# VectorE transposes k times its decay in blocks of 32 rows for the last 14 attention units, in place of TensorE's transposes and ScalarE's copy

## The chip, the cores and the metric

One core of a Trainium2 chip. The metric is the device time of one execution in microseconds (us), the median of several runs. The engines are TensorE (PE; its weight loads are listed as PEld), VectorE (DVE), ScalarE (ACT), GpSimd (POOL) and SyncE (SP), which issues the DMAs.

## The reference

Gated linear attention over 4 batches and 8 heads, and its output goes through a gated two-layer network:

```python
for t in range(S):                      # S = 768, D = 48, B = 4, H = 8
    state = alpha[:, :, t, :, None] * state + np.einsum('bhd,bhe->bhde', k[:, :, t], v[:, :, t])
    y[:, :, t] = np.einsum('bhd,bhde->bhe', q[:, :, t], state)
x = y.transpose(0, 2, 1, 3).reshape(B * S, H * D)          # 3072 x 384
gate = 1.0 / (1.0 + np.exp(-(x @ w_gate)))                 # 384 x 1536
out = (gate * (x @ w_val)) @ w_out                         # 1536 x 384
```

## The kernel before

The 3072 tokens are cut into 6 groups of 512. A group's attention is done in 4 units, one for each pair of heads, so there are 24 units, u = 0 to 23. The network is done in 72 steps, 12 for each group (one for each slice of 128 columns of the 1536). Every product of the network is taken three times with split operands, so a step is 27 matmuls of 128 by 128 by 512: nine for the gate (`pg`, L225), nine for the value (`pv`, L225), and six with `hh` and three with `hl` that add the step before into the three output banks (`po`, L643). For each step ScalarE takes the sigmoid (`sg`, L630), VectorE multiplies (L632), ScalarE writes the upper half `hh` (L634) and VectorE the lower half `hl` (L635). Gate and value use a ring of three PSUM banks, `r_three`, which the outputs of a unit share.

A unit of a later group runs while the network works on an earlier one. The first 8 units are `unit`, the others `late`. In `late` the two heads of a unit lie in rows 0 to 47 and 64 to 111 of a tile of 128 rows, with 512 tokens along it. VectorE scans the decays G (L381) and F (L385), GpSimd multiplies k by G in place (`kT`, L388), VectorE multiplies q by F into `A` (L549). `turn` then has TensorE transpose the four squares of 128 tokens of `kT` into the PSUM bank `pk` (L400), and ScalarE copies the bank to the tile `kn` (L404), which has the tokens along its rows. `scores` (L560) multiplies k and q, `adds` (L567) multiplies `kn` and v to give what each chunk of 64 tokens adds to the state. VectorE masks the scores (L573) and runs the states in eight dependent steps (L586), GpSimd scales them (L591). `outputs` of the unit (L603) come one unit later, right behind the next unit's `scores` and `adds`. ScalarE and VectorE take the outputs out of PSUM as `yt` (L422, L423), and DMAs from SP's queue put them in the tile `x` (L430), which the next group's gate and value products read.

The banks: `r_two` is a ring of two PSUM banks. A late unit takes three turns of it, the first for `pk` and two for `pas`, so `pk` and the second of `pas` are the same bank. `kn` is a ring of one tile once the early units have gone (`r_kn`), so a unit's `kn` can be written only when the `adds` of the unit before have read it.

The order of the work on each engine is set by a planner, class `Plan`. Every piece of work is given an engine, an estimated time, a due time (in steps of 6.12 us, from the dictionaries in `begin`) and what it reads and writes. The planner runs through time, and an engine that is free takes the piece with the earliest due time among those that are ready, where a piece's due time is also brought forward to what its users need. The network's pieces of steps after 14 that are marked `soon` go ahead of everything else. The order is then fixed, and each engine works through its list in that order. `last_step(u)` is the step beside which the outputs of unit u run, and y is three steps before it; the transposes are due at y - 0.5, the scores at y + 0.5, G of the next unit at y + 0.1.

Of the kernel before, what the change touches and what calls it, by code (L numbers as in the profile page):

```python
# [17 lines left out]
P = 128  # L18
# [18 lines left out]
CH, EH = T // C, T // E  # L37
X16 = R - D
PLACES = tuple((j * D + X16 * k, k, R * j + D, X16) for j in range(2) for k in range(NK)) + \
    tuple(((2 * p + j) * D, p - 1, R * j, D) for p in range(1, NP) for j in range(2))  # L40
EARLY = 2 * NP


WIDTH = EH + 3 * T + 1
# [143 lines left out]
def vec(n):  # L188
    return 0.07 + n / 960


def act(n):
    return 0.09 + n / 1180
# [35 lines left out]
def chunked(ctx, tc, rows, vc, vh, weights_in, out, const, ident, flags, weights, within):  # L229
    nc = tc.nc  # L230
    sb = ctx.enter_context(tc.tile_pool(name="sb", bufs=1))
    ps = ctx.enter_context(tc.tile_pool(name="ps", bufs=1, space=bass.MemoryType.PSUM))
    plan = Plan()
# [12 lines left out]
    def borrow(tag, *shape):  # L246
        t, at = slots[tag]
        size = 1
        for x in shape:
            size *= x  # L250
        slots[tag][1] = at + size
        name = f"{tag}_{at}"
        held[tag].append(name)
        t = t[:, at:at + size]
        if len(shape) == 2:
            t = t.rearrange("p (a b) -> p a b", b=shape[1])
        elif len(shape) == 3:
            t = t.rearrange("p (a b c) -> p a b c", b=shape[1], c=shape[2])
        return name, t
# [10 lines left out]
    def ring(name, n, *shape, dtype=F32, pool=None, early=()):  # L270
        return Ring([(f"{name}{i}", (pool or sb).tile([P, *shape], dtype, name=f"{name}{i}")) for i in range(n)], early)
# [5 lines left out]
    for _ in range(2):  # L277
        nm, t = borrow("w11", WF // 2, 2)
        raws.append((nm, t.bitcast(U32)))
    r_raw = Ring(raws)  # L280
    r_kn = ring("kn", 1, CH, P, early=[borrow("w6", CH, P) for _ in range(2)])
# [22 lines left out]
    r_two, r_three = Ring(r_at.tiles[:2]), Ring([*r_pg.tiles, *r_pv.tiles, r_at.tiles[2]])  # L304
# [9 lines left out]
    def later():  # L314
        nc.gpsimd.memset(d1g[E], 0.0)
        nc.gpsimd.memset(d1g[E][:, 0:T:E], 1.0)
        nc.gpsimd.memset(starts[:, 0:EARLY, CH:EH], 0.0)
        for lo in (0, E):
# [8 lines left out]
    plan.add("scalar", 0.7, None, picks, writes=[(pickn, "s")])  # L327
    plan.add("gpsimd", 1.5, NF - 4.0, later, writes=["later", *(("start", u) for u in range(EARLY))])

# [62 lines left out]
    def bound(u, t, fn, F):  # L392
        plan.add("scalar", act(T) + 0.22, t["flag"], lambda: nc.scalar.activation(
            out=F, in_=F, func=AF.Abs, accum_out=flags[:, u:u + 1]), writes=[fn, ("flag", u)])

    def turn(t, inn, kT, pkn, pk):

        def turned():
            for c in range(CH):
                nc.tensor.transpose(out=pk[:, c * P:(c + 1) * P], in_=kT[:, c * P:(c + 1) * P], identity=ident)  # L400

        plan.add("tensor", (0.109 * CH + 0.03, 0.9), t["X"], turned, [(inn, "k")], [pkn], fixed=True)
        knn, kn = r_kn.next()
        plan.add("scalar", act(CH * P), t["kn"], lambda: nc.scalar.copy(  # L404
            out=kn.rearrange("p c d -> p (c d)"), in_=pk[:, 0:CH * P]), [pkn], [knn])
        return knn, kn

    def finish(g, p, t, pyn, py):
# [26 lines left out]
    def unit(u, g, p, t):  # L435

        n, nch = T, CH
        bank = r_bank if u < NP else r_at
        inn, tin = r_in.next()
        for lo, hi, marks in ((0, A_K, "a"), (A_K, WIDTH, "rkq")) if u < 2 else ((0, WIDTH, "arkq"),):  # L440
            plan.add("sync", (0.475, P * (hi - lo) * 4 / RATE), t["load"], lambda lo=lo, hi=hi: nc.sync.dma_start(
                out=tin[:, lo:hi], in_=rows[g, p, :, lo:hi]), writes=[(inn, m) for m in marks])
        vn, v = r_v.next()
        plan.add("sync", (0.475, P * CH * 2 * D * 4 / RATE), after(t["load"], 0.2), lambda: nc.sync.dma_start(
            out=v.rearrange("p c j e -> p (c j e)"), in_=vc[g, p]), writes=[(vn, "v")])
        kT, qT = tin[:, A_K:A_Q], tin[:, A_Q:WIDTH]
# [3 lines left out]
            out=qT, in0=qT, in1=F, op=ALU.mult), [(inn, "r"), fn], [(inn, "q")], port=True)  # L450
        bound(u, t, fn, F)


        (pkn, pk), *pas = bank.next(), bank.next(), bank.next()
        knn, kn = turn(t, inn, kT, pkn, pk)

        def scores():
# [9 lines left out]
                                     start=True, stop=True)  # L467

        plan.add("tensor", (0.25 * nch + 0.1, 0.5), t["A"], scores, [(inn, "k"), (inn, "q")], [x[0] for x in pas])
        plan.add("tensor", (0.09 * nch + 0.1, 0.5), t["Y"], adds, [knn, (vn, "v")], [pkn])  # L470

        an, A = r_A.next()
        for j, (pan, pa) in enumerate(pas):
            plan.add("vector", vec(n), t["mask"], lambda pa=pa, j=j: nc.vector.tensor_tensor(
                out=A[:, j].rearrange("p (c t) -> p c t", t=C), in0=pa[:, 0:n].rearrange("p (c t) -> p c t", t=C),
# [17 lines left out]
        for lo in range(0, nch, some):  # L493
# [4 lines left out]
            out=sd, in0=st[:, 0:nch], in1=dec.rearrange("p (c o) -> p c o", o=1).broadcast_to([P, nch, D]), op=ALU.mult), [sn, decn], [(sdn, x) for x in range(4)])  # L498
# [30 lines left out]
    def late(u, g, p, t):  # L529


        inn, tin = r_in.next()
        plan.add("sync", (0.475, P * A_Q * 4 / RATE), t["load"], lambda: nc.sync.dma_start(
            out=tin[:, 0:A_Q], in_=rows[g, p, :, 0:A_Q]), writes=[(inn, m) for m in "ark"])
# [3 lines left out]
        for j in range(2):  # L538
            plan.add("sync", (0.475, R * T * 4 / RATE), after(t["load"], 0.1), lambda j=j: nc.sync.dma_start(
                out=A[own[j], j], in_=rows[g, p, own[j], A_Q:WIDTH]), writes=[(an, 2 + j)])  # L540
        plan.add("sync", (0.475, P * CH * 2 * D * 4 / RATE), after(t["load"], 0.2), lambda: nc.sync.dma_start(
            out=v.rearrange("p c j e -> p (c j e)"), in_=vc[g, p]), writes=[(vn, "v")])
        for j in range(2):
            plan.add("sync", (0.475, R * EH * D * 4 / RATE), after(t["load"], 0.3), lambda j=j: nc.sync.dma_start(
                out=vs[other[j], j].rearrange("p c e -> p (c e)"), in_=vh[g, p, j]), writes=[(vsn, j)])
        kT = tin[:, A_K:A_Q]
        fn, F, decn, dec = decays(u, E, t, inn, tin)
        for j in range(2):
            plan.add("vector", vec(T), t["q"], lambda j=j: nc.vector.tensor_tensor(  # L549
                out=A[own[j], j], in0=A[own[j], j], in1=F[own[j]], op=ALU.mult), [fn], [(an, 2 + j)], port=True)  # L550
        bound(u, t, fn, F)
        (pkn, pk), *pas = r_two.next(), r_two.next(), r_two.next()
        knn, kn = turn(t, inn, kT, pkn, pk)

        def scores():
            for c in range(EH):
# [10 lines left out]
                    nc.tensor.matmul(out=pas[c % 2][1][R * j:R * j + D, T // 2 + c // 2 * D:T // 2 + (c // 2 + 1) * D],  # L567
                                     lhsT=kn[ro, c // 2, R * j:R * j + D], rhs=v[ro, c // 2, j], start=True, stop=True)

        plan.add("tensor", (0.045 * EH, 0.5), t["Y"], adds, [knn, (vn, "v")], [x[0] for x in pas], fixed=True)  # L570
        for j, (pan, pa) in enumerate(pas):
            for i in range(2):
                plan.add("vector", vec(T // 2), t["mask"], lambda pa=pa, j=j, i=i: nc.vector.tensor_tensor(  # L573
                    out=A[other[j], j].rearrange("p (c i t) -> p i c t", i=2, t=E)[:, i],
# [5 lines left out]
        st, sn = sts[p], ("st", p)  # L580
        done = EH if u >= EARLY + NP else CH
        plan.add("gpsimd", 0.28, t["G"], lambda: nc.gpsimd.tensor_copy(out=st[:, 0, :], in_=st[:, done, :]), writes=[sn])
# [7 lines left out]
        for j in range(2):  # L590
            plan.add("gpsimd", pool_(EH * D), t["sd"], lambda j=j: nc.gpsimd.tensor_tensor(  # L591
                out=vs[own[j], j], in0=st[own[j], 0:EH], in1=dec[own[j]].rearrange("p (c o) -> p c o", o=1).broadcast_to([R, EH, D]), op=ALU.mult),
# [80 lines left out]
    def begin(u):  # L673
        g, p = divmod(u, NP)
        if u < EARLY:
            t = dict.fromkeys(("load", "G", "dec", "kt", "q", "X", "kn", "Y", "A", "mask", "S", "sd", "out", "y"))
            t.update(flag=14.0 + u, run=1, e_q="gpsimd")
        else:
            o = last_step(u)
            y = o - 3  # L680
            t = dict(load=y - 5, G=y - 2.9, dec=y - 2, kt=y - 2.7, flag=y + 1 + 0.5 * p, q=y - 2.0, X=y - 0.50, A=y + 0.50, kn=y - 1,
                     Y=y + 0.51, mask=y + 0.6, S=y + 0.55, sd=y + 0.7, out=o + 0.52, y=None)
        return unit(u, g, p, t) if u < EARLY else late(u, g, p, t)

# [12 lines left out]
    for s in range(NG * NF):  # L697
        step(s)
        if s in finished:
            u = finished[s]  # L700
# [6 lines left out]
    every, one, total = sb.tile([P, 1], F32, name="every"), sb.tile([P, 1], F32, name="one"), r_at.next()  # L707
    nc.vector.memset(one, 1.0)
    late, n_units = NG * NF - 4, NG * NP
    plan.add("scalar", 0.5, late, lambda: nc.scalar.activation(out=starts.rearrange("p u c -> p (u c)"), in_=starts.rearrange("p u c -> p (u c)"),  # L710
                                                               func=AF.Abs, accum_out=flags[:, n_units:n_units + 1]),
             [("start", x) for x in range(n_units)], [("flag", n_units)])
# [5 lines left out]
        out=within, in0=total[1][0:1, 0:1], scalar1=G_BOUND, scalar2=None, op0=ALU.is_le), [total[0]])  # L718
# [99 lines left out]
def laid_out(np, q, k, v, alpha, w_gate, w_val, w_out):  # L818
# [4 lines left out]
    for g in range(NG):  # L823
        size = C if g * NP < EARLY else E
        first[g, :, :, 0:T // size] = a[g, :, :, 0:T:size]
# [43 lines left out]
```

## Time and profile before

| | us |
|---|---|
| median of 3 runs | 556.48 (555.26 to 557.22) |
| the profiled execution | 556.98 |
| its span in the trace | 555.3 |
| TensorE busy in the span | 542.1 (98%) |
| VectorE busy | 335.0 (60%) |
| ScalarE busy | 183.9 (33%) |
| GpSimd busy | 100.5 (18%) |

The profile is of one execution; its span ends 1.7 us short of the time of its run. "Busy" is the time in which at least one instruction of the engine runs; for TensorE matmuls overlap, so its cost is read from start to start. Late units follow each other every 21.08 us.

### The profile page before, as it was taken

The numbers are of one execution on the slowest core, as the hardware profiler recorded it, in microseconds if no ns is written. First come the engines' busy times: TensorE is split into PE (matmuls) and PEld (weight loads), VectorE is DVE, ScalarE is ACT, GpSimd is POOL, SyncE is SP. The second block draws the span as 40 slices with busy tenths as digits, with TensorE's granted clock in tenths as the row PEclk, the third lists the DMA queues.
The fourth block names the chain that finished last, engine by engine and source line by source line (L and its number), as shares of the span: only waits on it lengthen the run. The fifth ranks groups of instructions, "written<-read, shape, count | busy, mean of one in ns | idle before, by whom it ended". The sixth has DMA issues, their size and how long they took to land.

```text
span 555.3 us, 10288 instructions
## 1 busy us (share of the span) xinstructions
PE 542.1 (98%) x4162; PEld 432.8 (78%) x4162; DVE 335.0 (60%) x648; ACT 183.9 (33%) x334; POOL 100.5 (18%) x133
## 2 busy tenths in 40 slices
PE   8999999999999999999999999999999999999994
PEld 4667776767888888888888888888888888888883
DVE  6889998899858457467467466476475342222221
ACT  2547767652322222322222322222332222221211
POOL 5711222142212112022022022022021010000000
PEclk9999999999999999999999999999999999999998
DMA  8537675644413213324124234024232011100001
GB/s 311 203 102 247 217 228 164 213 132 121 141 31 116 70 45 116 123 48 116 57 59 115 94 79 115 25 92 115 71 102 50 15 28 30 58 0 1 1 1 63
DMA packets 21449, 54.36 MB, mean 98 GB/s; under 512 B 3472, under 2 KB 8592, under 8 KB 21392
## 3 DMA queue, kind: packets, MB, share of 16 engines
q1 hardware_dynamic: 21392, 53.60, 31.6%
q8 instruction: 35, 0.57, 0.4%
q14 instruction: 22, 0.18, 0.1%
HBM read 41.01 MB, written 4.72 MB: 82 GB/s over the span
## 4 chain that ended last, share of the span: by engine, by line
PE 84%; DVE 6%; DMA 4%; ACT 3%; issue 1%; POOL 0%; SPq 0%; DVEq 0%; ACTq 0%; POOLq 0%
PE po L643 24%; PE pv L225 16%; PE pg L225 16%; PE at L225 15%; DMA raw<-in_w_dram 3%; PE pv L614 2%; PE at L560 2%; PE at L400 1%; PE pv L603 1%; PE at L567 1%; DVE w L355 1%; PE pg L603 1%; PE at L603 1%; DVE raw L351 1%; DMA first_w<-in_w_dram 1%
## 5 line engine op out<-in xcount | busy, mean ns | idle before, releaser
L225 PE MATMUL pg<-x,w 128*128 128x512 f32 x477 | 117.4, 390 | 0.0
L643 PE MATMUL po<-hh,w 128*128 128x512 f32 x432 | 115.7, 400 | 1.3 <-ACT hh L634 1.3
L225 PE MATMUL pv<-x,w 128*128 128x512 f32 x459 | 113.4, 391 | 0.7 <-DVE hl L635 0.7
L225 PEld LDWEIGHTS pg<-x,w 128*128 128x128 f32 x477 | 89.1, 188 | 19.1 <-issue 0.4
L225 PEld LDWEIGHTS pv<-x,w 128*128 128x128 f32 x459 | 85.5, 188 | 20.2 <-DVE hl L635 2.0
L643 PEld LDWEIGHTS po<-hh,w 128*128 128x128 f32 x432 | 78.2, 188 | 18.5 <-ACT hh L634 1.9
L225 PE MATMUL at<-x,w 128*128 128x512 f32 x360 | 88.3, 390 | 0.0
L225 PEld LDWEIGHTS at<-x,w 128*128 128x128 f32 x360 | 67.4, 188 | 14.2 <-issue 0.2
L591 POOL TENSOR_TENSOR vs<-st,dec 64x384 f32<-64x384 f32 x32 | 26.4, 827 | 213.0 <-DVE st L586 211.8
L643 PE MATMUL po<-hl,w 128*128 128x512 f32 x216 | 62.0, 392 | 0.0
L632 DVE TENSOR_TENSOR pv<-pv,sg 128x512 f32<-128x512 f32 x32 | 22.3, 697 | 53.9 <-PE pv L225 53.9
L388 POOL TENSOR_TENSOR in<-in,G 128x512 f32<-128x512 f32 x22 | 33.0, 1500 | 90.3 <-DVE G L381 42.1
L632 DVE TENSOR_TENSOR pg<-pg,sg 128x512 f32<-128x512 f32 x21 | 14.7, 699 | 56.2 <-PE pg L225 56.0
L643 PEld LDWEIGHTS po<-hl,w 128*128 128x128 f32 x216 | 40.2, 188 | 9.0 <-issue 0.4
L632 DVE TENSOR_TENSOR at<-at,sg 128x512 f32<-128x512 f32 x19 | 13.3, 699 | 53.0 <-PE at L225 53.0
L586 DVE SCALAR_TENSOR_TENSOR st<-st,dec,at 128x48 f32<-128x48 f32 x128 | 33.9, 265 | 8.4 <-PE at L567 3.0
L630 ACT ACTIVATE sg<-pg 128x512 f32<-128x512 f32 x32 | 19.2, 599 | 57.4 <-PE pg L225 57.4
L634 ACT CAST hh<-pv 128x512 fp32r<-128x512 f32 x32 | 18.9, 589 | 43.1 <-DVE pv L632 43.1
L630 ACT ACTIVATE sg<-at 128x512 f32<-128x512 f32 x21 | 12.6, 600 | 54.8 <-PE at L225 54.8
L630 ACT ACTIVATE sg<-pv 128x512 f32<-128x512 f32 x19 | 11.4, 600 | 52.5 <-PE pv L225 52.5
L381 DVE TENSOR_TENSOR_SCAN G<-in,d1g 128x512 f32<-128x512 f32 x22 | 26.7, 1215 | 2.0 <-DMA in<-in_rows_dram 1.8
L385 DVE TENSOR_TENSOR_SCAN F<-in,d1f 128x512 f32<-128x512 f32 x22 | 27.5, 1251 | 0.5
(158 smaller groups left out, 577.4 us busy)
## 6 DMA issues: line engine op xcount, KB each, us to landing
in<-in_rows_dram SPq DMA_DIRECT2D x16, 516.5 KB, 4.2
raw<-in_w_dram SPq DMA_DIRECT2D x12, 576.0 KB, 5.3
first_w<-in_w_dram SPq DMA_DIRECT2D x10, 576.0 KB, 5.0
x<-yt SPq DMA_DIRECT2D x30, 192.0 KB, 3.4
out_dram<-raw SPq DMA_DIRECT2D x18, 256.0 KB, 2.3
v<-in_vc_dram SPq DMA_DIRECT2D x22, 192.0 KB, 4.6
A<-in_rows_dram SPq DMA_DIRECT2D x32, 128.0 KB, 4.0
in<-in_rows_dram SPq DMA_DIRECT2D x4, 772.5 KB, 5.0
```

The costliest lines, as they stand in the source:

```text
L225: nc.tensor.matmul(out=dst, lhsT=lhs(a, i), rhs=rhs(b, i), start=(n == 0 and i == 0), stop=(n == len(todo) - 1 and i == NK - 1))
L381: plan.add("vector", scan(n), t["G"], lambda: nc.vector.tensor_tensor_scan(out=G[:, ::-1], data0=az[:, n:0:-1], data1=d1g[size], initial=0 ...
L385: plan.add("vector", scan(n), after(t["G"], 0.01), lambda: nc.vector.tensor_tensor_scan(out=F, data0=az[:, 0:n], data1=d1f, initial=0.0, o ...
L388: plan.add("gpsimd", pool_(n), t["kt"], lambda: nc.gpsimd.tensor_tensor(out=kT, in0=kT, in1=G, op=ALU.mult), [gn, (inn, "r")], [(inn, "k")])
L560: nc.tensor.matmul(out=pas[j][1][ro, c // 2 * E:(c // 2 + 1) * E], lhsT=kT[r, cs], rhs=A[r, j, cs], start=True, stop=True)
L586: nc.vector.scalar_tensor_tensor(out=st[:, c + 1, :], in0=st[:, c, :], scalar=dec[:, c:c + 1], in1=pas[c % 2][1][:, T // 2 + c // 2 * D:T ...
L591: plan.add("gpsimd", pool_(EH * D), t["sd"], lambda j=j: nc.gpsimd.tensor_tensor(out=vs[own[j], j], in0=st[own[j], 0:EH], in1=dec[own[j]]. ...
L603: nc.tensor.matmul(out=py[R * j:R * j + D, cs], lhsT=vs[r, j, c, :], rhs=A[r, j, cs], start=True, stop=True)
L630: plan.add("scalar", act(T), None, lambda: nc.scalar.activation(out=sg, in_=got["g"][1][:, 0:T], func=AF.Sigmoid), [got["g"][0]], [sgn], s ...
L632: plan.add("vector", vec(T), None, lambda: nc.vector.tensor_tensor(out=pv, in0=pv, in1=sg, op=ALU.mult), [sgn], [pvn], soon=soon)
L634: plan.add("scalar", act(T), None, lambda: nc.scalar.copy(out=hh, in_=pv), [pvn], [hhn], soon=soon)
L643: nc.tensor.matmul(out=pso_now[m][1][:, 0:T], lhsT=weights.part("o", b, f)[:, m * P:(m + 1) * P], rhs=h[a][:, 0:T], start=(f == 0 and i == ...
```

## The change

For units 10 to 23 `turn` isn't called. The tile `kn` is written by VectorE itself, straight from `kT`: for each block of 32 rows of `kT` (`a`) and each block of 32 tokens within the squares of 128 (`b`), one transpose instruction reads 32 rows by 4 by 32 elements and writes 32 rows by 4 by 32 elements; that is 16 instructions for a unit, put into the plan as four pieces of four. Units 0 to 9 keep TensorE's transposes and ScalarE's copy. A unit of the 14 takes two turns of the bank ring and not three. The plan is told of 4 x (0.07 + 128/960) us = 0.81 us for each piece.

```diff
+TURNED = 2
@@ turn
         plan.add("scalar", act(CH * P), t["kn"], lambda: nc.scalar.copy(
-            out=kn.rearrange("p c d -> p (c d)"), in_=pk[:, 0:CH * P]), [pkn], [knn])
+            out=kn.rearrange("p c d -> p (c d)"), in_=pk[:, 0:CH * P]), [pkn], [(knn, a) for a in range(4)])
@@ unit (and in the same way late): adds
-        plan.add("tensor", (0.09 * nch + 0.1, 0.5), t["Y"], adds, [knn, (vn, "v")], [pkn])
+        plan.add("tensor", (0.09 * nch + 0.1, 0.5), t["Y"], adds, [*((knn, a) for a in range(4)), (vn, "v")], [pkn])
@@ late
-        (pkn, pk), *pas = r_two.next(), r_two.next(), r_two.next()
-        knn, kn = turn(t, inn, kT, pkn, pk)
+        if u < EARLY + TURNED:
+            (pkn, pk), *pas = r_two.next(), r_two.next(), r_two.next()
+            knn, kn = turn(t, inn, kT, pkn, pk)
+        else:
+            pas = r_two.next(), r_two.next()
+            knn, kn = r_kn.next()
+            blocks = kT.rearrange("p (c q t) -> p q c t", q=4, t=32)
+            for a in range(4):
+                def turned(a=a):
+                    for b in range(4):
+                        nc.vector.transpose(out=kn[32 * b:32 * b + 32, :, 32 * a:32 * a + 32], in_=blocks[32 * a:32 * a + 32, b])
+
+                plan.add("vector", 4 * vec(P), t["X"], turned, [(inn, "k")], [(knn, a)], port=False)
```

## Rows read from the trace of the kernel before

**Rows 1.** The page: busy time by engine, and the chain that ended last
```profile
PE 542.1 (98%) x4162; PEld 432.8 (78%) x4162; DVE 335.0 (60%) x648; ACT 183.9 (33%) x334; POOL 100.5 (18%) x133
PE 84%; DVE 6%; DMA 4%; ACT 3%; issue 1%; POOL 0%; SPq 0%; DVEq 0%; ACTq 0%; POOLq 0%
```
**Rows 2.** Busy time by stretch, one late unit each; then PEclk, DMA share, GB/s
```profile
168.20:189.28 21.08, 21.08 (x189) 17.41 (x189) 12.56 (x26) 5.36 (x10) 4.07 (x5) 1.00 0.25 76
...
379.00:400.08 21.08, 21.08 (x184) 17.25 (x185) 13.16 (x27) 6.44 (x12) 3.75 (x4) 1.00 0.37 113
```
**Rows 3.** Timeline of PE, 412 to 446 us: start, time, engine, line
```profile
412.42 2.21 PE L225 MATMUL at<-x,w 128*128 128x512 f32 x9
414.47 0.60 PE L400 MATMUL at<-ident,in 128*128 128x128 f32 x4
414.82 1.63 PE L643 MATMUL po<-hh,w 128*128 128x512 f32 x6
416.30 0.84 PE L643 MATMUL po<-hl,w 128*128 128x512 f32 x3
...
421.66 0.54 PE L567 MATMUL at<-v,kn 64*48 64x48 f32 x32
...
427.38 2.20 PE L225 MATMUL pv<-x,w 128*128 128x512 f32 x9
429.42 1.52 PE L643 MATMUL po<-hh,w 128*128 128x512 f32 x6
430.77 0.84 PE L643 MATMUL po<-hl,w 128*128 128x512 f32 x3
```
**Rows 4.** Groups by line: ACT's copy (busy, mean ns, idle before)
```profile
L404 ACT COPY kn<-at 128x512 f32<-128x512 f32 x21 | 12.4, 591 | 33.2 <-PE at L400 33.2
```
**Rows 5.** Timeline of DVE, one period; in brackets the idle time before
```profile
401.15 2.43 DVE L586 SCALAR_TENSOR_TENSOR st<-st,dec,at 128x48 f32<-128x48 f32 x8 [0.21 <-PE at L567]
403.50 0.68 DVE L635 TENSOR_TENSOR hl<-pg,hh 128x512 fp32r<-128x512 f32 x1
...
405.97 0.69 DVE L423 TENSOR_TENSOR yt<-pv,yt 128x512 fp32r<-128x512 f32 x1
406.58 1.22 DVE L381 TENSOR_TENSOR_SCAN G<-in,d1g 128x512 f32<-128x512 f32 x1
...
410.11 0.69 DVE L635 TENSOR_TENSOR hl<-pg,hh 128x512 fp32r<-128x512 f32 x1
...
414.74 0.70 DVE L632 TENSOR_TENSOR at<-at,sg 128x512 f32<-128x512 f32 x1 [2.37 <-PE at L225]
416.21 0.69 DVE L635 TENSOR_TENSOR hl<-at,hh 128x512 fp32r<-128x512 f32 x1 [0.77 <-ACT hh L634]
421.32 0.70 DVE L632 TENSOR_TENSOR pv<-pv,sg 128x512 f32<-128x512 f32 x1 [4.42 <-PE pv L225]
```
**Rows 6.** Timeline of POOL in the same period: k times its decay
```profile
408.02 1.50 POOL L388 TENSOR_TENSOR in<-in,G 128x512 f32<-128x512 f32 x1 [2.87 <-DVE G L381]
```
**Rows 7.** Groups by line and shape: DVE instructions of other sizes
```profile
L387 DVE TENSOR_TENSOR dec<-in,G 128x8 f32<-128x8 f32 x16 | 2.6, 164 | 0.0
L573 DVE TENSOR_TENSOR A<-at,mask 64x256 f32<-64x256 f32 x64 | 27.0, 422 | 1.1
L549 DVE TENSOR_TENSOR A<-A,F 64x512 f32<-64x512 f32 x32 | 22.5, 702 | 0.5
```
**Rows 8.** Timeline of all engines at the end of a group's attention
```profile
216.10 0.69 DVE L423 TENSOR_TENSOR yt<-pv,yt 128x512 fp32r<-128x512 f32 x1
216.82 1.18 SPq L430 DMA_DIRECT2D x<-yt  x2
220.50 2.28 PE L225 MATMUL pv<-x,w 128*128 128x512 f32 x9
220.91 1.45 PEld L225 LDWEIGHTS pv<-x,w 128*128 128x128 f32 x7 [0.21 <-issue]
```
**Rows 9.** Line L430 in 210 to 225 us: from issue to landing
```profile
DMA to landing us min/median/max: 3.2/3.3/3.4
```

## What the change will do to the time

> **What bounds the kernel now.** First the busy times and the chain that ended last: TensorE is busy for 98% of the span and makes 84% of the chain; VectorE is busy for 60% [rows 1]. These are means over unlike stages, so the second view is the busy time by stretches. I cut the stretch from 168 to 442 us at the period of the late units, 21.08 us; it gives 13 stretches, and they hold the transposes of all but the first of the 14 units that change, which stand in the period ahead. In every one TensorE is busy for the whole 21.08 us at a granted clock of 1.00, while VectorE is busy for 12.56 us, or up to 13.16 us in the periods where it also copies a result out [rows 2]. So in this region time is TensorE's instruction stream and nothing else: an instruction taken out of it shortens the kernel by its own spacing, and one put on another engine costs nothing as long as TensorE isn't made to wait. The third view is the timeline of TensorE, for that spacing; the fourth that of VectorE, for the holes that have to take the new work.
>
> **What is removed.** Durations of matmuls overlap, so I read from start to start across the same three blocks, once with the transposes and once without. With them, from the first product of the nine at 412.42 to the first `hl` product at 416.30: 3.88 us. Without them, 427.38 to 430.77: 3.39 us [rows 3]. The difference is 0.49 us; of it 0.35 us lie between the first transpose (414.47) and the next product (414.82), and the rest is a slower change-over around them. The periods at 343 to 353 and 427 to 438 us, read in the same way, give 0.48. For 14 units: 14 x 0.48 = 6.7 us off TensorE's stream. ScalarE loses a copy of 0.59 us a unit [rows 4]. ScalarE is busy for 5.4 us of 21 [rows 2], so this is worth nothing in time. The shared PSUM bank and the third turn of the ring go too; no wait in this region comes from them, since TensorE has no idle time there, so they are worth nothing either.
>
> **What is added.** 16 transpose instructions a unit on VectorE, each over 32 rows and 128 elements a row. No instruction of that kind is in the trace, so the price c of one, from start to start, is bounded by its neighbours. Below: an instruction of 8 elements takes 0.164 us, nearly all of it fixed cost. Above: 512 elements a row take 0.702 us; in between, 256 elements read from PSUM take 0.422 us [rows 7]. The line from 8 to 512 elements rises by 0.538 us in 504 elements, 0.00107 us each; at 128 it stands at 0.164 + 120 x 0.00107 = 0.29 us, and at 256 at 0.43, near the middle row. [...] For the range I keep 0.16 (2.6 us) and 0.70 (11.2 us), the latter if blocks are not streamed.
>
> [...]
>
> Does it fit? After the change a period is 21.08 - 0.48 = 20.60 us. VectorE needs 12.56 + 4.8 = 17.4 us, plus about 1.0 us in which it waits whatever the order (0.21 for the `adds`, 0.77 for `hh` [rows 5]): 18.4 us, and 0.6 more in a copying period. It fits with some 2 us to spare. The holes are there: 4.42, 2.37 and 0.77 us in the period shown [rows 5].
>
> **Where it lands in the queue, and who waits behind it.** A unit's transposes may run from the time when the `adds` of the unit before have read `kn` until its own `adds`, a whole period later. Their source is long ready: GpSimd writes `kT` in the period before [rows 6]. By due times, states, mask and `yt` stand ahead of them, and so do the network's own pieces; G and F of the next unit are due later and get pushed behind them. So I expect four groups of four after `yt`, at a place like 406.6 [rows 5], with q times F and the network's pieces between them, and the scans some 4 to 5 us later, in what are now the holes. Behind the scans stands GpSimd's `kT` of the next unit: now it begins at 408.02 [rows 6], then at about 413, and it is wanted only after the burst at 421.66 [rows 3]. `adds` wait for the last transpose, at about 413, eight us ahead of need. A multiply or an `hl` of the network can come up to one group, 1.2 us, late. The `hl` that ends at 410.80 [rows 5] is first read by the product at 416.30 [rows 3], so 5.5 us cover that; if the cover were gone, each lost us would cost 14 us over the kernel. The plan counts 0.81 us for a group that I price at 1.2; the lag is 1.6 us a period, less than the spare time, so it doesn't add up. SP's queue gets nothing new.
>
> **The sum.** The profiled execution took 556.98 us; less 6.7 is 550.3. The median of the runs is 0.5 us below that execution, so the forecast for the median is 556.48 - 6.7 = 549.8 us, 1.2% faster.
>
> **The rivals.**
> (1) *VectorE becomes the bound.* One mechanism: the price c of a transpose. TensorE waits as soon as 12.56 + 16c + 1.0 is over 20.60, that is from c = 0.44 us, and the kernel is slower than before when it is over 21.08, from c = 0.47 us. Halfway between the rows of 256 and of 512 elements lies 0.56 us: a period of 22.5 us, 1.9 x 14 = 26 us more than the 550, or 576 us. For it speaks that two of my three rows lie at or near the limit, that each instruction uses a quarter of the rows, and that the rows change from one instruction to the next; against it, that 128 elements are the smallest of those sizes and that the fixed cost in the rows is only 0.16 us. [...] Chance of slower than before 0.13.
> (2) *VectorE just full:* c of 0.43 to 0.47, some part of the gain lost in waits, 554 to 557 us. Two passes over the 128 elements, 0.43 us by the line above, would do this. Chance 0.08.
> (3) *A group gets ahead of `yt`.* The last unit of each group has no slack: `yt` ends at 216.79, its second DMA issue ends at 218.00, and 3.3 us later [rows 9] the third product of the group beginning at 220.50 may start, which already takes 0.07 us longer than usual, with 0.21 us idle on its loads [rows 8]. Any delay of `yt` there goes straight to TensorE. Three of the 14 periods are such (outputs of units 11, 15 and 19). One group ahead costs 3 x 1.2 = 3.6 us: 553.4 us. Against it: `yt` is due before the product that reuses its bank, half a step ahead of the transposes. Chance 0.09.
> (4) *The gap is only filled by another wait:* the product behind the transposes at 414.82 would wait for `hh`. Its `hh` is from the step before, as the `hl` above, so I give it no chance of its own.
>
> **How the numbers follow.** The forecast (549.8; its own range 548 to 551, the spread of the runs being about 1 us to each side) has 0.70, the rivals 0.13, 0.08 and 0.09. What a measurement can tell from no change is 0.3%, 1.7 us: faster means under 554.8. Faster: 0.70 and nearly all of rival 3, 0.78. Within: rival 2 and a little, 0.09. Slower: 0.13. A low price c below 0.30 adds no gain, since hidden work is hidden, so the low end is 548.0. The high end takes in rival 3 with a margin, 554.2; the upper bound of c stays outside it with rivals 1 and 2, which is the 2 in 10 left out.
>
> **What would show it.** Right: the late periods are 20.6 us; TensorE is still busy all through them; L400 is gone after unit 9 and the `hh` product follows 2.04 us after the start of the nine; VectorE shows 16 transposes a unit of about 0.3 us, a busy time of some 17 us a period, all ended several us before the `adds`. Wrong: transposes of over 0.44 us, a VectorE without holes, and TensorE idle with VectorE as releaser at L567 (`adds`), L643 or L225 (rival 1 or 2); or TensorE idle at L225 at the start of groups 2, 3 and 4 alone, with `yt` behind a group of transposes (rival 3).

## The result and the profile after

The changed kernel takes 550.44 us (median of 4 runs, 550.17 to 552.02) against 555.92 us of the kernel before (4 runs; with three of them it was 556.48); the ratio is 0.9889, with a 95% interval from 0.9864 to 0.9915. That is 5.5 us, or 1.1%. The forecast was 549.8 us, with 6.7 us off. So the mechanism held, and 1.2 us of the gain didn't come; where they went is read off below.

The page first: busy time by engine, then the chain that ended last. In the changed file most lines have moved by 1 to 12: the transposes are L563, the products into `po` L655 (before L643), gate and value L226 (L225), `adds` L579 (L567), the multiply L644, `hl` L647, the states L598.

```profile
PE 535.9 (98%) x4106; PEld 427.5 (78%) x4106; DVE 404.1 (74%) x872; ACT 176.4 (32%) x320; POOL 102.4 (19%) x133
PE 85%; DVE 7%; DMA 3%; ACT 2%; issue 1%; POOL 0%; SPq 0%; DVEq 0%; ACTq 0%; POOLq 0%
```

TensorE is as full as before, at 98%, and has lost 56 transposes (4162 instructions are now 4106); VectorE has gone from 60 to 74% [rows 1]. By stretches, cut at the new period (start and end, length, then busy time of PE, PEld, DVE, ACT and POOL, granted clock, DMA share, GB/s):

```profile
167.30:187.90 20.60, 20.60 (x182) 17.01 (x181) 17.55 (x42) 4.86 (x9) 4.23 (x5) 1.00 0.26 78
...
373.30:393.90 20.60, 20.60 (x178) 16.92 (x177) 18.23 (x43) 5.84 (x11) 4.00 (x4) 1.00 0.36 105
```

The period is 20.60 us where it was 21.08, and TensorE is busy in all of it, at a granted clock of 1.00. VectorE has gone from 12.56 to 17.55 us [rows 2]. On TensorE's timeline (start, time, engine, line) a step without transposes now follows where they stood:

```profile
406.62 2.20 PE L226 MATMUL at<-x,w 128*128 128x512 f32 x9
408.66 1.52 PE L655 MATMUL po<-hh,w 128*128 128x512 f32 x6
410.02 0.84 PE L655 MATMUL po<-hl,w 128*128 128x512 f32 x3
410.70 2.20 PE L226 MATMUL pg<-x,w 128*128 128x512 f32 x9
```

From the nine to the first `hl` product it is 3.40 us, which was 3.88 with the transposes [rows 3]; the `hh` product follows 2.04 us behind the start of the nine, as forecast. The groups by line give the price of the new instruction (busy, mean ns of one, idle before), and VectorE's timeline shows where the pieces stand in a period:

```profile
L563 DVE STREAM_TRANSPOSE kn<-in 32x128 f32<-32x128 f32 x224 | 67.7, 302 | 3.3
```
```profile
400.18 0.69 DVE L424 TENSOR_TENSOR yt<-pv,yt 128x512 fp32r<-128x512 f32 x1
400.79 1.24 DVE L563 STREAM_TRANSPOSE kn<-in 32x128 f32<-32x128 f32 x4
402.06 1.41 DVE L550 TENSOR_TENSOR A<-A,F 64x512 f32<-64x512 f32 x2
403.49 1.25 DVE L563 STREAM_TRANSPOSE kn<-in 32x128 f32<-32x128 f32 x4
404.77 0.70 DVE L644 TENSOR_TENSOR pg<-pg,sg 128x512 f32<-128x512 f32 x1
405.50 2.52 DVE L563 STREAM_TRANSPOSE kn<-in 32x128 f32<-32x128 f32 x8
408.06 0.69 DVE L647 TENSOR_TENSOR hl<-pg,hh 128x512 fp32r<-128x512 f32 x1
408.67 1.21 DVE L382 TENSOR_TENSOR_SCAN G<-in,d1g 128x512 f32<-128x512 f32 x1
...
413.47 0.69 DVE L647 TENSOR_TENSOR hl<-at,hh 128x512 fp32r<-128x512 f32 x1 [0.99 <-ACT hh L646]
414.08 0.16 DVE L388 TENSOR_TENSOR dec<-in,G 128x8 f32<-128x8 f32 x1
415.05 0.70 DVE L644 TENSOR_TENSOR pv<-pv,sg 128x512 f32<-128x512 f32 x1 [0.81 <-PE pv L226]
```

One transpose takes 0.302 us, and eight follow each other in 2.52 us, so the spacing is (2.52 - 0.302) / 7 = 0.317 us. The pieces stand behind `yt`, as expected, with q times F and the network's multiply and `hl` between them. Of the holes of 4.42 and 2.37 us [rows 5] 0.81 us are left of the first and nothing of the second; the wait for `hh`, 0.77 us before, is 0.99. The row to keep in mind is the `hl` at 408.06: it ends at 408.75, and TensorE begins the product that reads it at 410.02. The slack of 5.5 us has come down to 1.27.

**Where the 1.2 us went.** I read the start of each unit's `adds` on TensorE's timeline and took the differences. From unit 9's to unit 10's it was 22.21 us before and is 22.80 after: the first unit on VectorE made its period longer. The 13 periods behind it are 20.60 us, or up to 20.81 where a group begins. TensorE's timeline and VectorE's in that place:

```profile
151.69 1.52 PE L655 MATMUL po<-hh,w 128*128 128x512 f32 x6
154.09 2.35 PE L226 MATMUL pg<-x,w 128*128 128x512 f32 x9 [0.88 <-DVE hl L647]
```
```profile
150.03 0.70 DVE L644 TENSOR_TENSOR pg<-pg,sg 128x512 f32<-128x512 f32 x1
150.63 1.24 DVE L563 STREAM_TRANSPOSE kn<-in 32x128 f32<-32x128 f32 x4
151.91 1.41 DVE L550 TENSOR_TENSOR A<-A,F 64x512 f32<-64x512 f32 x2
153.34 0.69 DVE L647 TENSOR_TENSOR hl<-pg,hh 128x512 fp32r<-128x512 f32 x1
```

A piece of four stands ahead of an `hl`, and TensorE waits 0.88 us for it, because the product wants the bank that this `hl` reads. In the kernel before, the same `hl` and the same product:

```profile
152.78 0.69 DVE L635 TENSOR_TENSOR hl<-pg,hh 128x512 fp32r<-128x512 f32 x1
153.53 2.32 PE L225 MATMUL pg<-x,w 128*128 128x512 f32 x9
```

This `hl` ended at 153.47, so its slack was 0.06 us, where the one in the prediction had 5.5. VectorE isn't full in this period: it was busy for 13.03 of 22.21 us before and is for 17.57 of 22.80 after. But it works without a pause from 145.2 to 159.7 us, and this `hl` lies in that stretch. Summed over the periods: 13 x 0.48 = 6.2 us won, 0.6 lost in unit 10's, and about 0.2 lost in the three periods in which a group begins; 5.4 us, where the medians differ by 5.5. The rest of the two spans, 555.3 and 548.4 us, differs in the first 130 us, in which the order on every engine is the same: unit 8's `adds` begin at 128.58 us in the one and 127.18 in the other, and at 127.1 to 131.1 in the profiles of other kernels with that same beginning. That is a difference between executions and not one of the change.

### The profile page after: what moved, and what is told of

Same layout as the page of the kernel before. It is cut to its first block, busy times and chain, and to the rows that moved or that the text cites. A ratio compares the mean times of both kernels' runs of the same rounds, so it can differ in the third digit from the quotient of the medians.

```text
span 548.4 us, 10383 instructions
## 1 busy us (share of the span) xinstructions
PE 535.9 (98%) x4106; PEld 427.5 (78%) x4106; DVE 404.1 (74%) x872; ACT 176.4 (32%) x320; POOL 102.4 (19%) x133
## 4 chain that ended last, share of the span: by engine, by line
PE 85%; DVE 7%; DMA 3%; ACT 2%; issue 1%; POOL 0%; SPq 0%; DVEq 0%; ACTq 0%; POOLq 0%
PE po L655 24%; PE pv L226 17%; PE pg L226 16%; PE at L226 15%; PE pv L626 2%; DMA raw<-in_w_dram 2%; PE at L572 2%; PE pv L615 1%; PE pg L615 1%; PE at L615 1%; PE at L579 1%; DVE w L356 1%; DVE st L598 1%; DVE raw L352 1%; DVE hl L647 1%
## 5 line engine op out<-in xcount | busy, mean ns | idle before, releaser
L226 PE MATMUL pg<-x,w 128*128 128x512 f32 x477 | 117.4, 390 | 0.9 <-DVE hl L647 0.9
L655 PE MATMUL po<-hh,w 128*128 128x512 f32 x432 | 113.9, 396 | 0.6 <-ACT hh L646 0.5
L226 PE MATMUL pv<-x,w 128*128 128x512 f32 x459 | 113.4, 391 | 0.7 <-DVE hl L647 0.7
L226 PEld LDWEIGHTS pg<-x,w 128*128 128x128 f32 x477 | 89.1, 188 | 20.1 <-DVE hl L647 1.3
L226 PEld LDWEIGHTS pv<-x,w 128*128 128x128 f32 x459 | 85.5, 188 | 20.0 <-DVE hl L647 1.8
L655 PEld LDWEIGHTS po<-hh,w 128*128 128x128 f32 x432 | 79.2, 188 | 18.7 <-ACT hh L646 1.3
L226 PE MATMUL at<-x,w 128*128 128x512 f32 x360 | 88.3, 390 | 0.0
L226 PEld LDWEIGHTS at<-x,w 128*128 128x128 f32 x360 | 67.4, 188 | 14.2 <-issue 0.2
L563 DVE STREAM_TRANSPOSE kn<-in 32x128 f32<-32x128 f32 x224 | 67.7, 302 | 3.3
L389 POOL TENSOR_TENSOR in<-in,G 128x512 f32<-128x512 f32 x22 | 29.6, 1343 | 188.9 <-issue 98.2
L655 PE MATMUL po<-hl,w 128*128 128x512 f32 x216 | 62.1, 392 | 0.0
L655 PEld LDWEIGHTS po<-hl,w 128*128 128x128 f32 x216 | 40.2, 188 | 8.8 <-issue 0.4
L644 DVE TENSOR_TENSOR pv<-pv,sg 128x512 f32<-128x512 f32 x32 | 22.2, 694 | 31.2 <-PE pv L226 30.9
L598 DVE SCALAR_TENSOR_TENSOR st<-st,dec,at 128x48 f32<-128x48 f32 x128 | 33.8, 264 | 8.0 <-PE at L579 3.0
L644 DVE TENSOR_TENSOR pg<-pg,sg 128x512 f32<-128x512 f32 x21 | 14.6, 694 | 33.0 <-PE pg L226 32.7
L644 DVE TENSOR_TENSOR at<-at,sg 128x512 f32<-128x512 f32 x19 | 13.2, 693 | 29.9 <-PE at L226 29.8
L386 DVE TENSOR_TENSOR_SCAN F<-in,d1f 128x512 f32<-128x512 f32 x22 | 32.7, 1485 | 0.1
L646 ACT CAST hh<-pg 128x512 fp32r<-128x512 f32 x21 | 12.3, 587 | 54.3 <-DVE pg L644 54.3
```

Of the source, the lines that this page charges most:

```text
L226: nc.tensor.matmul(out=dst, lhsT=lhs(a, i), rhs=rhs(b, i), start=(n == 0 and i == 0), stop=(n == len(todo) - 1 and i == NK - 1))
L386: plan.add("vector", scan(n), after(t["G"], 0.01), lambda: nc.vector.tensor_tensor_scan(out=F, data0=az[:, 0:n], data1=d1f, initial=0.0, o ...
L389: plan.add("gpsimd", pool_(n), t["kt"], lambda: nc.gpsimd.tensor_tensor(out=kT, in0=kT, in1=G, op=ALU.mult), [gn, (inn, "r")], [(inn, "k")])
L563: nc.vector.transpose(out=kn[32 * b:32 * b + 32, :, 32 * a:32 * a + 32], in_=blocks[32 * a:32 * a + 32, b])
L598: nc.vector.scalar_tensor_tensor(out=st[:, c + 1, :], in0=st[:, c, :], scalar=dec[:, c:c + 1], in1=pas[c % 2][1][:, T // 2 + c // 2 * D:T ...
L644: plan.add("vector", vec(T), None, lambda: nc.vector.tensor_tensor(out=pv, in0=pv, in1=sg, op=ALU.mult), [sgn], [pvn], soon=soon)
```

## The experiments

The table gives for each run, from its trace, the period of unit 10 (from unit 9's `adds` to its own) and the usual period of the 13 units behind it; the time is the median, with the ratio to the kernel before on the same chip (for the one timed once, none).

| kernel | unit 10 | usual period | us | ratio (95%) |
|---|---|---|---|---|
| before | 22.21 | 21.08 | 555.92 | 1 |
| after | 22.80 | 20.60 | 550.44 | 0.9889 (0.9864 to 0.9915) |
| e1, VectorE's load alone | 23.22 | 21.07 | 557.66 | 1.0015 (0.9996 to 1.0035) |
| e2, no transposes for units 10 to 23 | 21.70 | 20.60 | 551.03 | 0.9898 (0.9855 to 0.9940) |
| e3, 32 on VectorE | 27.68 | 27.33 | 641.47 | 1.1506 (1.1462 to 1.1550) |
| e4, 24 on VectorE | 24.96 | 22.21 | 574.46 | 1.0303 (1.0274 to 1.0331) |
| e9, 24 in small pieces | 22.66 | 20.60 | 558.50 | 1.0035 (1.0019 to 1.0051) |
| e5, units 8 and 9 too | 23.06 | 20.60 | 557.24 | 0.9997 (0.9979 to 1.0015) |
| e11, unit 9 too, small pieces | 23.64 | 20.60 | 553.75 | 0.9946 (0.9922 to 0.9970) |
| e6, from unit 11 on | 22.21 | 20.60 | 551.98 | 0.9922 (0.9901 to 0.9944) |
| e7, plan told the true price | 22.30 | 20.60 | 551.32 | 0.9895 (0.9870 to 0.9919) |
| e10, small pieces | 22.16 | 20.60 | 550.69 | 0.9900 (0.9865 to 0.9934) |
| e8, one wide transpose | see there | 20.60 | 550.88 | one run |

### The two halves of the change, each alone

VectorE's load without TensorE's relief. `extra` is a piece of memory that is idle by then:

```diff
-            pas = r_two.next(), r_two.next()
-            knn, kn = r_kn.next()
+            (pkn, pk), *pas = r_two.next(), r_two.next(), r_two.next()
+            knn, kn = turn(t, inn, kT, pkn, pk)
...
-                        nc.vector.transpose(out=kn[32 * b:32 * b + 32, :, 32 * a:32 * a + 32], in_=blocks[32 * a:32 * a + 32, b])
+                        nc.vector.transpose(out=extra[32 * b:32 * b + 32, :, 32 * a:32 * a + 32], in_=blocks[32 * a:32 * a + 32, b])
```

The rest of the edit gives the pieces the name of this tile and lets `adds` wait for them, as they do in the changed kernel.

> TensorE's transposes and ScalarE's copy stay for all 24 units, and VectorE makes its 16 transposes a unit for units 10 to 23 as well, into a tile that nobody reads: VectorE's load alone. Theory (TensorE's stream sets the time, VectorE's transposes are hidden): late periods of 21.08 us as before, with VectorE at 17.5 us in each; in all the 555.9 us of the kernel before, plus up to 1 us once, in unit 10's period, where VectorE has no holes: 556 to 557. Rival (the transposes cost time in every period, and the change gained only what TensorE's saving left over): periods over 21.08, 559 us or more.

The stretches of this run:

```profile
358.50:379.57 21.07, 21.07 (x194) 17.40 (x190) 17.53 (x43) 5.46 (x10) 4.24 (x5) 1.00 0.26 76
```

VectorE is at 17.53 us, as in the changed kernel, and the period is that of before, 21.07. Unit 10's period grew by 1.01 us, the three in which a group begins by less than 0.1 us each. Now TensorE's relief without VectorE's load:

```diff
-            blocks = kT.rearrange("p (c q t) -> p q c t", q=4, t=32)
-            for a in range(4):
-                ...
-                plan.add("vector", 4 * vec(P), t["X"], turned, [(inn, "k")], [(knn, a)], port=False)
```

> The changed kernel without any transpose for units 10 to 23: kn keeps what unit 9 left in it, so the states and outputs of these units are computed from a stale tile. TensorE's saving alone. Theory: periods of 20.60 us, the same as with VectorE's transposes, and unit 10's period without its loss: 555.9 - 14 x 0.48 = 549.2 us, about 1 us below the changed kernel's 550.4. Rival (VectorE's transposes cost time in every period): periods under 20.60, 547 us or less.

```profile
357.00:377.60 20.60, 20.60 (x179) 17.01 (x178) 12.88 (x27) 4.87 (x9) 4.07 (x5) 1.00 0.26 74
```

The period is 20.60 with VectorE at 12.88 us, and 20.60 with it at 17.55. So in the ten regular periods 4.7 us of VectorE's work cost nothing at all, and the 0.48 us are TensorE's spacing alone. In the three in which a group begins they cost at most 0.13 us (20.81, 20.67 and 20.70 us with the transposes, 20.68, 20.70 and 20.69 without). In unit 10's period they cost 22.80 - 21.70 = 1.10 us. In time the run is no faster than the changed kernel beyond the spread of the runs; its expected 1 us is read from the periods only.

### How much VectorE can take

The same order as in the changed kernel, with each instruction issued twice, or every second one twice:

```diff
-                    for b in range(4):
+                    for b in (0, 0, 1, 1, 2, 2, 3, 3):
```

> Each of VectorE's 16 transposes is issued twice, in the same plan order as in the changed kernel: 32 a unit. At the measured spacing of 0.316 us they take 10.1 us. Theory (VectorE becomes the bound once its work and 1.0 us of waits are over 20.60): 12.7 + 10.1 + 1.0 = 23.8 us a period, 3.2 us more in 13 periods, 592 us. Rival (the waits get filled, VectorE's work alone counts): 22.8 us, 579 us. Rival (TensorE's slack of several us soaks it up): 551 us.

```diff
-                    for b in range(4):
+                    for b in (0, 0, 1, 2, 2, 3):
```

> Half as many transposes again, 24 a unit, in the changed kernel's order: 7.6 us, which is what 16 of 0.47 us would take, the price from which the prediction has the kernel slower than before. Theory with 1.0 us of waits: 12.7 + 7.6 + 1.0 = 21.3 us a period, 0.7 more than 20.60 in 13 periods, 559 us. Rival (the waits get filled): 20.3 us, hidden, 550 to 551 us.

Both came out slower than any of the theories said, so this is the miss to learn from. One stretch of the run with 24, then its timeline:

```profile
292.21:314.43 22.22, 20.90 (x179) 16.93 (x178) 19.95 (x51) 4.77 (x10) 4.23 (x5) 1.00 0.25 72
```
```profile
317.02 3.88 DVE L563 STREAM_TRANSPOSE kn<-in 32x128 f32<-32x128 f32 x12
...
318.93 1.52 PE L655 MATMUL po<-hh,w 128*128 128x512 f32 x6
320.93 0.69 DVE L647 TENSOR_TENSOR hl<-pv,hh 128x512 fp32r<-128x512 f32 x1
...
321.67 0.97 PE L655 MATMUL po<-hl,w 128*128 128x512 f32 x3 [1.22 <-DVE hl L647]
322.48 2.21 PE L226 MATMUL pv<-x,w 128*128 128x512 f32 x9
```

VectorE isn't full: it is busy for 19.95 of 22.22 us. What costs is one place. The waits of TensorE that its trace shows from 200 to 400 us, nine periods, are all of one kind (us in total, times, longest):

```profile
PE po L655 <- DVE hl L647: 11.7, 9, 1.3
```

The `hl` stands behind all 24 transposes of its unit, and twelve of them without a break directly ahead of it; it ends at 321.6, and TensorE has waited 1.22 us. In the changed kernel this same `hl` had 1.27 us of slack; 8 more transposes bring 8 x 0.32 = 2.5 us, and 2.5 - 1.27 is 1.3. From the first `hh` product to the products behind `hl` it is 3.55 us here (318.93 to 322.48) and 2.04 in the changed kernel (408.66 to 410.70), so 1.51 of the 1.61 us that a period is longer are lost at this place. With 32 it is 16 x 0.32 - 1.27 = 3.9 us, and the wait is 3.70:

```profile
301.78 1.65 PE L655 MATMUL po<-hl,w 128*128 128x512 f32 x3 [3.70 <-DVE hl L647]
303.22 3.96 PE L226 MATMUL at<-x,w 128*128 128x512 f32 x9
307.02 2.24 PE L226 MATMUL pg<-x,w 128*128 128x512 f32 x9
```

There the wait costs a second time: behind it nine products take 3.96 us, and the next nine 2.24. The granted clock of such a period is 0.88, a mean. In stretches of 1 us it is 1.00 up to 300 us, 0.56 from 300 to 301 and 0.50 from there to 306: it fell within the wait, when TensorE had been idle since 298.1. To see whether it is the order and not VectorE's capacity, the 24 transposes once more, as 24 pieces of the plan, so that the planner can put an `hl` between them:

```diff
-            for a in range(4):
-                def turned(a=a):
-                    for b in range(4):
-                        nc.vector.transpose(...)
-                plan.add("vector", 4 * vec(P), t["X"], turned, [(inn, "k")], [(knn, a)], port=False)
+            for a in range(4):
+                for b in (0, 0, 1, 2, 2, 3):
+                    plan.add("vector", 0.316, t["X"], lambda a=a, b=b: nc.vector.transpose(...), [(inn, "k")], [(knn, a)], port=False)
```

> Again 24 transposes a unit, but each is a piece of the plan by itself, told at 0.316 us, so that the network's hl stands behind about ten of them and not behind all 24. Theory (in the run with half as many again it was the order that cost 1.6 us a period: the hl behind the last twelve came 1.3 us late for its product, while VectorE still had 2 us idle): periods of 20.6 to 20.9 us, 551 to 555 us. Rival (a full VectorE): about 22.2 us a period again, 574 us.

Ten of the 13 periods are 20.60 to 20.64 us, where 24 transposes took 22.21 before, and VectorE is busy for 19.4 us of them; so the order it was. (The size of the pieces and the price that the plan is told change together here; no run separates the two for 24.) The other three are 22.11, 24.76 and 22.56 us, and this I hadn't expected: with them the run takes 558.50 us and not 551 to 555. They are the periods in which TensorE passes to the next group. TensorE's longest waits from 200 to 400 us (us in total, times, longest), then lines of the second of the three, whose `adds` begin at 293.73:

```profile
PE po L653 <- ACT hh L644: 1.4, 1, 1.4
PE at L226 <- DMA x<-yt: 1.1, 1, 1.1
PE pv L226 <- DMA x<-yt: 0.7, 1, 0.7
```
```profile
301.93 0.69 DVE L424 TENSOR_TENSOR yt<-at,yt 128x512 fp32r<-128x512 f32 x1
...
304.06 0.29 PE L570 MATMUL at<-A,in 48*64 48x64 f32 x2 [0.37 <-issue]
304.73 0.69 PE L570 MATMUL at<-A,in 48*64 48x64 f32 x30 [0.38 <-DVE A L550]
...
307.20 3.18 PE L226 MATMUL at<-x,w 128*128 128x512 f32 x7 [1.12 <-DMA x<-yt]
```

With so much work VectorE reaches the states late: a scan and an `hl`, from 295.66 to 297.73 in the second period, now stand ahead of them. So `yt` begins 7.3 and 8.2 us behind `adds` in the first two of the three periods, where it is 5.4 in the changed kernel, and the next group's first products wait for `x`, 0.7 and 1.1 us. In other periods `yt` is as late, 6.3 to 7.8 us, and nobody waits for it. In the second period `scores` wait too, and the seven products behind the wait for `x` take 3.18 us; the granted clock of that period is 0.93. In the third it is an `hh` that is late, 1.4 us. The waits for `x` are the place of rival 3, which opens only once VectorE is that full.

### Unit 10, and the units before it

> VectorE transposes from unit 11 on, 13 units; unit 10 stays with TensorE. In the changed kernel unit 10's period took 22.80 us against 22.21 before, with TensorE waiting 0.88 us for an hl. Theory (the loss belongs to unit 10's place, where VectorE has no holes yet): that period is 22.21 again, the others stay at 20.60: 0.6 us faster than the changed kernel, 549.8 us. Rival (whichever unit is the first on VectorE pays): unit 11's period has the loss, 0.5 us slower than the changed kernel, 550.9 us.

```diff
-TURNED = 2
+TURNED = 3
```

Unit 10's period is 22.21 us again, and unit 11's, now the first on VectorE, is 20.60. So the loss belongs to the place and not to being first. It is not that VectorE is full there, as e6's expectation has it: VectorE was idle for 9.2 of the 22.21 us before, and it is the slack of 0.06 us that is missing. Part of the loss can also be taken out where it arises, in the order. The plan believed 0.81 us of a piece that takes 1.27:

```diff
-                plan.add("vector", 4 * vec(P), t["X"], turned, [(inn, "k")], [(knn, a)], port=False)
+                plan.add("vector", 4 * 0.316, t["X"], turned, [(inn, "k")], [(knn, a)], port=False)
```

> The plan is told the measured price, 4 x 0.316 = 1.26 us for a piece of four transposes, and not 0.81; nothing else is changed. Theory (unit 10's loss comes from a piece that the plan put ahead of an hl because it took it for cheaper than it is): TensorE's wait of 0.88 us for that hl goes, at most 1.1 us faster than the changed kernel, 549.4 us. Rival (the order comes out the same, or the loss is that of a full VectorE): 550.4 us.

and in 16 pieces (the diff is that of e9, with `for b in range(4)`, and each of the 16 has a name of its own that `adds` wait for):

> The changed kernel with its 16 transposes as 16 pieces of the plan, each told at 0.316 us. Theory: late periods of 20.60 us as in the changed kernel, since nothing waits there; in unit 10's period the hl is no longer behind four of them, and its 22.80 us fall to 21.7 to 22.3: 549.3 to 549.9 us where the changed kernel has 550.4. Rival (unit 10's loss is that of a full VectorE): 22.8 us again.

They bring unit 10's period to 22.30 and 22.16 us, so 0.5 to 0.6 of its 1.10 us was the order. In place of 0.88 us TensorE waits 0.2 us for an `hl` with 16 pieces; with the true price that wait is gone, and there is one of 0.4 us for a `sg`. The rest of the loss stays in both. In the medians none of the three differs from the changed kernel: all the intervals overlap. Half a microsecond is below what these runs can tell, and I don't claim a faster version.

Towards the front it goes the other way:

> VectorE transposes for units 8 and 9 too, 16 units in all. These two lie at 100 to 150 us, where VectorE is busy for 22.5 of 24.5 us. Theory (a transpose is free only where VectorE has holes): two units bring 2 x 5.06 us of VectorE work into some 4 us of holes, TensorE waits for VectorE there, 3 us slower than the changed kernel: 553.5 us. Rival (only TensorE's stream counts): 2 x 0.48 us faster, 549.4 us.

```diff
-TURNED = 2
+TURNED = 0
```

> The same in pieces of one, with unit 9 on VectorE too: 15 units. Unit 9 lies at 128 to 147 us, where VectorE is busy for 22.5 of 24.5 us. Theory (no holes there): the 17.78 us from unit 8's adds to unit 9's or the period behind grow by more than the 0.48 that TensorE saves, about 2 us: 551 to 552 us. Rival (with small pieces the order avoids the loss): 0.48 us less than with 14 units, 549 us.

With all 16 late units the gain is gone, 557.24 against 557.03 us of before: a loss twice as large as expected. Most of it lies ahead of unit 8's `adds`, which begin at 134.18 us here and at 127.1 to 131.1 in all other runs. VectorE, busy for 23.6 of 24.5 us from 122.5 to 147, then works through weights, scans and transposes at once, and TensorE waits in several places for pieces that come late. Its waits from 115 to 145 us:

```profile
PE po L655 <- ACT hh L646: 1.9, 2, 1.2
PE pg L226 <- DVE w L356: 0.6, 1, 0.6
PE pg L515 <- ACT sg L642: 0.5, 1, 0.5
```

ScalarE isn't the cause though it is named: `hh` waits for VectorE's multiply (the `hh` at 120.56 us for 1.03 us). With unit 9 alone, in small pieces, unit 9's period grows from 17.78 to 19.66 us and unit 10's is 23.64; half the gain is left, again less than expected.

### The price of a transpose

> One transpose instruction over 128 rows and 512 elements in place of the 16 small ones. Its blocks stay in their own 32 rows, so kn isn't the transpose that adds needs, and the states come out other than the reference. What it is for: the price of an instruction by its length. If a 4-byte element takes one cycle, as in the multiplies of the same rows (0.702 us for 512 elements): 0.66 to 0.73 us. If an element takes two: about 1.2 us. If nearly all of the 0.302 us of a small one is fixed: under 0.5 us. Time of the kernel: 549 to 551 us.

```diff
-            for a in range(4):
-                ...
+            def turned():
+                nc.vector.transpose(out=kn.rearrange("p c d -> p (c d)"), in_=kT)
+
+            plan.add("vector", 16 * vec(P), t["X"], turned, [(inn, "k")], [(knn, a) for a in range(4)], port=False)
```

```profile
L561 DVE STREAM_TRANSPOSE kn<-in 128x512 f32<-128x512 f32 x14 | 9.8, 703 | 0.1
```

703 ns for 512 elements and 302 for 128 make 401 / 384 = 1.044 ns for an element and 168 ns fixed, if the number of rows, 128 in the one and 32 in the other, makes no difference; no run separates it from the length. At 512 elements that is the price of a multiply of the same length, 702 ns [rows 7]. No trace shows VectorE's clock, so how many cycles an element takes isn't told by this; in time it is the first of the three expected ranges. (In this run the plan put unit 10's `adds` earlier, so that its period, 15.50 us, and unit 11's, 26.94, can't be compared with the others.)

## Why the prediction was right, and where it wasn't

**What is removed.** Right to the hundredth in ten of the periods: 0.48 us a unit; 0.34 to 0.46 in the three in which a group begins. It is the spacing and not the duration that counts: the four transposes last 0.60 us together [rows 3].

**What is added.** Right: 0.302 us for one and 0.317 from start to start, where the straight line between two rows of other operations gives 0.29; e8 shows why it works: a transpose of 512 elements takes 0.703 us and a multiply of as many 0.702 [rows 7]. The forecast took 0.30 for one, so 4.8 us for 16 and 1.2 us for a group of four, and no run shows a ground for going above the line; what the runs showed in their place is 0.317 us from start to start, so 5.1 us for 16, in which VectorE is busy for 4.84 us, and 1.24 to 1.25 us for four. VectorE's sum, 17.4 us, came out at 17.55.

**Where it goes and who waits.** The place was right (behind `yt`, the scans behind the transposes), and `kn` is ready several us ahead of `adds`. Two sizes were wrong. The scan of G starts 13.3 us after the states' start where it was 5.4, so it moved by 7.9 us and not by 4 to 5, because the multiply, the `hl` and q times F are pushed ahead of it too. And "up to one group, 1.2 us, late" for an `hl` was wrong by a factor of three: it lost 5.5 - 1.27 = 4.2 us, since all 16 transposes stand ahead of it. In the changed kernel that is still covered. But it means that the point at which TensorE begins to wait isn't c = 0.44 us, where VectorE's work fills the period, but by an estimate from the slack that is left 0.317 + 1.27 / 16 = 0.40, where one `hl` in the fixed order is late; e4 and e3 show it by waits of 1.22 and 3.70 us. The step that failed there is rival 1's, in using a sum of busy times for an engine that works through a fixed order. For small pieces the sum is nearly right: e9 has 20.60 us with VectorE busy for 19.4 us.

**The sum.** 14 x 0.48 was the term that was mis-sized, for the 14th unit. I read the cover of one `hl`, 5.5 us, in one regular period and took all 14 periods for the same; in unit 10's an `hl` had 0.06 us. That period lost 0.59 us where the sum has it gain 0.48: 1.07 us, which is most of the 1.2 us by which the gain falls short. e2 and e6 show this loss by taking it away, e10 by taking away 0.64 us of it. That 549.8 lies only 0.64 us from 550.44 is in part luck: the median of the kernel before fell by 0.56 us with its fourth run.

**The rivals.** The prices of rivals 1 and 2 didn't occur; rival 1's threshold is told above. Rival 3 was right in its place: the three periods in which a group begins are 20.81, 20.67 and 20.70 us, 0.07 to 0.21 over the others, where before it was 0.05 to 0.07. But no piece got ahead of `yt`, which begins 5.4 us behind `adds` before and after; and without any transposes (e2) these periods are 0.08 to 0.10 over the others. In e9 it had waits of 0.7 and 1.1 us.

## What to carry to other kernels

Where one engine's instruction stream is the bound, take work out of it even if another engine needs ten times as long for it (0.48 us against 5.06), as long as that engine has holes in the same stretch. Check the holes in every period that the work goes into (units 8 and 9 had too few), and check not only the sum of the busy times: with a fixed order, find in each period the piece on the critical engine's path that stands behind the new work, and count its slack. It was 5.5 us in the period that I read and 0.06 us in the first one that was changed. And give the planner small pieces at their measured price, which is what turned 22.21 us into 20.60 for the same 24 transposes in ten of 13 periods.

## What the runs showed that was not expected

A wait of TensorE of 3.70 us cost some 2.5 us more behind it: nine products took 3.96 instead of 2.20 us, three took 1.65 instead of 0.84, at a granted clock of 0.50. In e4 one wait of 1.22 us in each period left the clock at 1.00. In e9 three waits close together, 0.37, 0.38 and 1.12 us from 303.7 to 307.2, did not: in stretches of 1 us the granted clock is 1.00 up to 306, 0.83 in the next and 0.50 from 307 to 310. So the length of the longest wait alone doesn't tell whether the clock falls. And the first 130 us of a kernel can differ by 4 us between executions with the same order of work, which is most of a 1% effect: such an effect is read from periods in the traces better than from spans.
